# An attention-and-Mish kernel on one core: three kinds of elementwise work move from VectorE to GpSimd, and the written order changes

## The chip, the cores and the metric

The kernel runs on one core of one Trainium2 chip. The metric is device time in microseconds of one execution. Three executions of the kernel before took 684.23, 684.58 and 684.82 us, and the median, 684.58, is the time to compare with. The profile names the engines PE (TensorE matmuls), PEld (TensorE weight loads), DVE (VectorE), ACT (ScalarE), POOL (GpSimd) and SP (the queue that issues most DMAs).

## The reference

```python
def _A_ref(x, wqkv, wo):                       # x: 1 x 2048 x 640, 32 heads of 20 columns
    qkv = (x @ wqkv).reshape(B, S, 3, H, Dh).transpose(2, 0, 3, 1, 4)
    q, k, v = qkv[0], qkv[1], qkv[2]
    p = softmax(einsum("bhqd,bhkd->bhqk", q, k) * Dh ** -0.5, axis=-1)
    return einsum("bhqk,bhkd->bhqd", p, v).transpose(0, 2, 1, 3).reshape(B, S, D) @ wo
def _B_ref(x, w1, b1, w2):                     # 640 -> 1536 -> 640
    h = x @ w1 + b1
    return (h * tanh(softplus(h))) @ w2        # Mish
g = sigmoid((x * gate_w).sum(-1))
return g * _A_ref(x, wqkv, wo) + (1 - g) * _B_ref(x, w1, b1, w2)
```

All inputs and the output are bfloat16.

## The kernel before

The attention is cut into 32 groups. A group is four heads (a "quad", eight of them) and 512 query rows (four chunks). A group has 16 key tiles of 128 keys; a tile times a head is one score unit, so there are 16 x 4 x 32 = 2048 score units. A score matmul (L1119) uses 32 rows of the PE array, so that up to four of different rows run side by side, and it fills one PSUM bank of 128 x 512.

The exponential of a unit is made in one of two ways. In 1380 units ScalarE does it (`x`, L1137), one to three banks in an instruction, into the ring E. In the other 668 units (167 tiles, called `d` sets) VectorE does it by arithmetic on the bits (`power_of`, L615): it writes 16-bit integers which, read as bfloat16, are an approximate power of two. Such an approximation is made better by averaging copies with different offsets. A copy with an offset is an integer addition over the whole set, 128 x 2048 bfloat16 read as 512 words of 64 bits, and GpSimd does it (`add_shift`, L645, two additions for each set, 334 in all). 151 of the sets ("three") keep three copies: the first is multiplied with V (tile VA), the other two with V scaled by a constant (tile VD). The other 16 ("two") let VectorE add two copies (L669) and use two. The set's tiles are nine buffers named T0 to T8 in the code.

The multiplication with V (`V`, L1154) takes four matmuls side by side, one head each, 21 columns wide: 20 of V and a column of ones, so that the sum of the exponentials comes out with the result. It adds up in one PSUM bank, `acc`. When a group's last `V` is done, `normalise` follows: `a` transposes `acc` in blocks of 32 into T1 on VectorE (L1183), `b` takes the reciprocal of the sums (L1190), `c` multiplies 128 x 320 floats of T1 by it into the bfloat16 tile T2 (L1197), and four DMAs store T2 to `o_dram`. For the last two groups of the last chunk a further transpose takes the place of the DMAs or, in the very last group, of `c` also.

VD is made once for a quad: `make_vd` (step `v`) queues two VectorE instructions (L597), one for each constant, over 128 x 588 bfloat16. Seven of a quad's sixteen key tiles have a scaled V. The other work is matrix products in `chains`: q, k and v projections, the hidden layer (48 evacuations with the bias, L882), the second layer (L924) and the output projection (L998). The bias arrives as bfloat16 in `b1bf` and is cast to floats in `b1f` ahead of the first evacuation of the hidden layer (L881).

Nothing is scheduled automatically. The string `ORDER` is the whole program order, the outcome of a search. `S n,bank` makes n score units, `D` one score unit of a `d` set, `x n` an exponential over n banks, `V j,i` the product of tile j (i = -1 from E, 0 to 2 from the copies of a set), `C`, `F`, `f` work on a chain, `d` opens a set. VectorE's and GpSimd's instructions are put into two numbered lists when they become possible (`dve`, `gps`), and `y n` or `p n,tag` emits entry n; the tag says which T buffer an addition writes, or -1 for none or in place. Each engine executes its own instructions strictly in the order in which they were emitted, and waits for semaphores in that order.

Of the kernel before, what the change touches and what calls it, by code (L numbers as in the profile page):

```python
# [19 lines left out]
S2,5 x2 S2,2 S2,0 C0,4 C1,5 C2,6 F0 F0 F0 F0 F0 F1 y1 F y3 x2 C3,5 S1,2 y4 S1,3 C4,6 x2 x2 F3 F S1,0 y5 S1,1  # L20
C6,5 F F d1,2,0 F F y2 F d0,0,0 x2 F S1,3 y6 x1 S1,2 S1,4 F F F F x1 C5,6 F6 F6 F6 F F6 F F F F6 F6 x1 F6 C7,0
F6 F6 F6 C8,4 y7 S3,1 x2 F7 F5 F7 F7 y8 y9 F7 F F7 y10 y12 S2,1 x1 y11 S2,5 V1,-1 F F F F C9,3 d1,7,0 V0,-1 F8
F8 F8 y13 F8 F8 x2 F F8 F8 F8 F8 S3,0 F8 F8 F8 F8 x2 F8 F8 F x3 F F y14 F S2,5 V2,-1 x2 V3,-1 S1,0 y15 S1,1
y16 y17 C11,5 S1,2 y18 y19 S2,3 C10,6 x3 V4,-1 F F11 F11 F11 F11 F11 F11 F F F11 F F S1,1 q1 S1,2 V5,-1 x2 F11
F11 y20 v0,0 F11 F11 F11 F11 S1,0 C12,3 x2 S1,4 D0,15,3,6 F11 F11 F11 F11 F11 x1 F11 F F11 x1 F y23 S2,1
D0,15,0,0 y24 d3,4,0 d0,6,0 y25 y26 y27 F y28 x2 D0,15,2,5 S1,4 y29 S1,6 F V6,-1 F x1 y30 x1 l3 y31 S1,0 S1,2
x1 C13,5 F F S1,6 x1 S1,3 D0,14,3,1 S1,4 C14,0 F13 F x1 F F13 F13 F y32 y33 F F F V7,-1 S2,1 D0,15,1,6 y34 F F
F F x2 F F F F D0,14,0,5 S2,3 V8,-1 F F y35 F F F x2 D0,14,1,6 S2,1 y36 F V9,-1 C15,6 y37 y38 y39 x2 V10,-1
S3,3 x2 F F y40 F x3 F y41 l2 F F F F D0,14,2,2 y22 S2,0 y21 p1,8 V15,0 F F V11,-1 S1,5 y42 S1,3 y43 V14,0 y44
# [308 lines left out]
def kernel(  # L338
# [12 lines left out]
    nc = tc.nc  # L351
# [236 lines left out]
    def make_vd(p, part):  # L588
# [14 lines left out]
        for i in range(NSH):  # L603
            dve(lambda i=i: scale(i))
# [256 lines left out]
    def h_chain(ft, c, start, due):  # L861
# [14 lines left out]
        def evac(ch):  # L876
            ps = ch.ps

            def copy():
                if (ft, c) == (0, 0):  # L880
                    nc.vector.tensor_copy(b1f, b1bf)  # L881
# [563 lines left out]
```

## Time and profile before

| | us | share of the span |
|---|---|---|
| profiled execution | 685.2 | |
| its span (first to last instruction) | 683.4 | |
| PE busy | 674.0 | 99% |
| ACT busy | 667.9 | 98% |
| DVE busy | 603.0 | 88% |
| POOL busy | 356.8 | 52% |

The profiled execution took 685.2 us, of which 683.4 us lie between its first and its last instruction; 0.6 us more than the median of the three timed runs. The granted TensorE clock was 1.000 over the whole span. Busy times of an engine are unions: a matmul's record lasts until its modelled end and overlaps the next one's, so 99% says that PE was never long without a matmul in flight, and not that it streamed at its peak. The groups by line give, for each kind of instruction, the number, the busy time, the mean duration, and the idle time that its engine spent just before instructions of the kind, with what ended it.

### The profile page before, as it was taken

What the parts mean: (1) busy time and instruction counts of PE and PEld (TensorE: products, weight loads), DVE (VectorE), ACT (ScalarE), POOL (GpSimd) and SP (SyncE); (2) the same over time, 40 slices, a digit from 0 to 9 for tenths busy, and PEclk for the clock granted to TensorE, in tenths of its full rate; (3) what the DMA queues carried; (4) which work ended last, traced back from release to release, by engine and by line L of the source; (5) the groups of instructions that cost most, each with busy time, mean ns of one, the idle gap of its engine ahead of it and who ended that gap; (6) DMA issues with size and microseconds to landing.
All of it is one profiled execution on the core that took longest, in us unless ns stands there. A gap on an engine that the chain in (4) does not pass through costs nothing.

```text
span 683.4 us, 24492 instructions
## 1 busy us (share of the span) xinstructions
PE 674.0 (99%) x10339; PEld 236.7 (35%) x10339; DVE 603.0 (88%) x1037; ACT 667.9 (98%) x695; POOL 356.8 (52%) x349
## 2 busy tenths in 40 slices
PE   8999999999999999999999999999999999999997
PEld 4433332323333443333333223222243333333333
DVE  5688989899999889999889988999998988899896
ACT  6999999999999999999999999999999999999995
POOL 5045555454454535575555545456645655565543
PEclk9999999999999999999999999999999999999999
DMA  7443422214312121112132113321322113162231
GB/s 170 99 100 94 89 49 71 49 34 93 74 25 53 38 48 27 26 39 38 44 92 42 34 58 89 46 70 28 58 55 73 19 30 64 25 82 43 56 86 59
DMA packets 128542, 40.47 MB, mean 59 GB/s; under 512 B 94960, under 2 KB 127872, under 8 KB 128432
## 3 DMA queue, kind: packets, MB, share of 16 engines
q1 hardware_dynamic: 126032, 38.29, 25.5%
q8 instruction: 81, 1.33, 0.8%
q10 hardware_dynamic: 2400, 0.62, 0.4%
q14 instruction: 29, 0.24, 0.1%
HBM read 22.29 MB, written 12.78 MB: 51 GB/s over the span
## 4 chain that ended last, share of the span: by engine, by line
PE 81%; ACT 12%; DVE 3%; issue 3%; DMA 1%; POOL 0%; SPq 0%; DVEq 0%; POOLq 0%; ACTq 0%
PE Sp L699 27%; PE Sp L1119 26%; PE Sp L1154 26%; ACT E L1137 12%; DVE T L615 1%; DMA wf<-in_A_wqkv_dram 1%; PE Sp L688 0%; DVE T L669 0%; DVE st L784 0%; DVE T L1197 0%; POOL T L645 0%; PE Sp L1384 0%; PE Sp L1169 0%; DVE ot L1401 0%; PE Sp L1263 0%
## 5 line engine op out<-in xcount | busy, mean ns | idle before, releaser
L1137 ACT ACTIVATE E<-Sp 128x1024 bf16<-128x1024 f32 (+2 forms) x677 | 635.9, 1090 | 3.5 <-PE Sp L1119 2.7
L645 POOL INT64_ADD T<-T x334 | 347.0, 1050 | 311.7 <-DVE T L615 180.1
L615 DVE TENSOR_SCALAR T<-Sp 128x512 int16<-128x512 f32 x668 | 438.1, 684 | 49.8 <-PE Sp L1119 41.0
L1119 PE MATMUL Sp<-qT,kT 32*128 32x512 bf16 x2048 | 260.9, 383 | 1.9 <-DVE T L615 0.9
L1119 PEld LDWEIGHTS <-kT 32*128 32x128 bf16 x2048 | 69.5, 91 | 234.1 <-issue 229.2
L1154 PE MATMUL Sp<-E,VA 128*21 128x512 bf16 x1380 | 129.5, 382 | 0.0
L1154 PE MATMUL Sp<-T,VD 128*21 128x512 bf16 x1272 | 117.6, 382 | 0.1
L699 PE MATMUL Sp<-w_sb,big 128*32 128x320 bf16 x1508 | 77.1, 302 | 0.3 <-DVE T L615 0.2
L699 PE MATMUL Sp<-xT,w1t 128*32 128x512 bf16 x952 | 75.0, 382 | 0.0
L1154 PEld LDWEIGHTS <-VA 128*21 128x21 bf16 x2048 | 44.8, 90 | 62.8 <-issue 55.5
L1154 PE MATMUL Sp<-T,VA 128*21 128x512 bf16 x668 | 64.1, 382 | 0.0
L699 PE MATMUL Sp<-xT,ws 128*32 128x512 bf16 x720 | 56.6, 382 | 0.3 <-DVE VA L838 0.2
L699 PEld LDWEIGHTS <-big 128*32 128x32 bf16 x1508 | 34.0, 95 | 30.3 <-issue 21.2
L1154 PEld LDWEIGHTS <-VD 128*21 128x21 bf16 x1272 | 31.1, 90 | 36.8 <-issue 29.8
L882 DVE TENSOR_SCALAR big<-Sp,b1f 128x512 bf16<-128x512 f32 x48 | 35.6, 742 | 2.2 <-PE Sp L699 1.8
L699 PE MATMUL Sp<-wv,xT 128*32 128x81 bf16 (+2 forms) x960 | 34.8, 257 | 0.0
L699 PE MATMUL Sp<-wo_sb,od 128*32 128x320 bf16 (+1 forms) x604 | 30.3, 300 | 0.0
L699 PEld LDWEIGHTS <-w1t 128*32 128x32 bf16 x952 | 21.5, 94 | 25.2 <-issue 18.0
L784 DVE CAST st<-Sp 128x512 bf16<-128x512 f32 x36 | 24.4, 684 | 2.8 <-PE Sp L699 2.1
L1183 DVE STREAM_TRANSPOSE T<-Sp 128x512 f32<-128x512 f32 x32 | 22.7, 709 | 2.2 <-PE Sp L1154 2.0
L699 PEld LDWEIGHTS <-xT 128*32 128x32 bf16 x960 | 20.6, 96 | 11.3 <-issue 5.9
L699 PEld LDWEIGHTS <-ws 128*32 128x32 bf16 x720 | 17.1, 95 | 19.1 <-issue 12.5
(82 smaller groups left out, 222.5 us busy)
## 6 DMA issues: line engine op xcount, KB each, us to landing
w1t<-in_B_w_dram SPq DMA_DIRECT2D x24, 320.0 KB
q_dram<-st SPq DMA_DIRECT2D x20, 128.0 KB
b_dram<-bt SPq DMA_DIRECT2D x16, 160.0 KB
bl<-b_dram SPq DMA_DIRECT2D x16, 160.0 KB
qT<-q_dram SPq DMA_DIRECT2D x124, 20.0 KB
o_dram<-T SPq DMA_DIRECT2D x120, 20.0 KB
out_dram<-ot SPq DMA_DIRECT2D x15, 160.0 KB
kT<-k_dram SPq DMA_DIRECT2D x28, 80.0 KB
```

The lines of the kernel that those rows point to most:

```text
L615: nc.vector.tensor_scalar(out=dst.bitcast(I16), in0=src, scalar1=inv_sqrt_dh * LOG2E * 128.0, scalar2=127.0 * 128.0 + (BETA2 if two else B ...
L645: nc.gpsimd.int64_add(dst[:, :].bitcast(I64), src[:, :].bitcast(I64), n * 0x0001000100010001)
L699: nc.tensor.matmul(out_[k : k + 32], lhsT=lhsT[:, k : k + 32], rhs=rhs, tile_position=(0, k), start=start, stop=ch.done(), skip_group_chec ...
L784: nc.vector.tensor_copy(out=res["st"][:, :], in_=ps[:, :])
L882: nc.vector.tensor_scalar(out=big[:, pair_of(c, ft), (ft % 2) * QC : (ft % 2 + 1) * QC], in0=ps[:, :], scalar1=b1f[:, ft : ft + 1], scalar ...
L1119: nc.tensor.matmul(ps_cols, lhsT=kT[p][32 * t_ : 32 * t_ + 32, j * P : (j + 1) * P], rhs=qT[G][32 * t_ : 32 * t_ + 32, :], tile_position=( ...
L1137: nc.scalar.activation(E[:, x : x + n, :], allb[:, k0 : k0 + n, :], ACT.Exp, scale=inv_sqrt_dh,)
L1154: nc.tensor.matmul(acc[32 * t_ : 32 * t_ + DH + 1, :], lhsT=lhsT, rhs=rhs, start=(pv_done[G] == 0), stop=(pv_done[G] == pv_total[G] - 1), ...
L1183: nc.vector.transpose(out=st["T1"][:, :, :].rearrange("p b r -> p (b r)"), in_=acc[:, :])
```

## The change

Three things move from VectorE's list to GpSimd's.

- `c` of `normalise`, in 31 of the 32 groups: the product of T1 and the reciprocals (L1197) becomes a GpSimd instruction. It is queued when `b` is emitted, and its DMAs (or the last transpose) follow it as before.
- `scale` of `make_vd`, 16 instructions (L597).
- the cast of the bias, one instruction: it is queued right behind the bias's load (the step `l2`), and no longer stands in the first evacuation of the hidden layer.

```diff
@@ load_late @@
                 nc.sync.dma_start(b1bf, B_b1.rearrange("(ft p) -> p ft", p=P))
+                gps(lambda k: nc.gpsimd.tensor_copy(b1f, b1bf))
@@ make_vd @@
         def scale(i):
-            nc.vector.tensor_scalar(
+            nc.gpsimd.tensor_scalar(
                 out=VD[p][:, lo - (NS - ND) : hi - (NS - ND), i, :],
...
         for i in range(NSH):
-            dve(lambda i=i: scale(i))
+            gps(lambda k, i=i: scale(i))
@@ h_chain @@
             def copy():
-                if (ft, c) == (0, 0):
-                    nc.vector.tensor_copy(b1f, b1bf)
                 nc.vector.tensor_scalar(
@@ normalise @@
         def a_done():
-            dve(b, (lambda: dve(ends)) if G == NG - 1 else (lambda: dve(c, c_done)))
+            dve(b, (lambda: dve(ends)) if G == NG - 1 else (lambda: gps(lambda k: (c(), c_done()))))
...
         def c():
-            nc.vector.tensor_tensor(
+            nc.gpsimd.tensor_tensor(
                 out=T2[i][:, :].rearrange("p (b r) -> p b r", r=32)[:, :, 0:DH],
@@ ORDER, 303 lines become 306; the first of each @@
-S2,5 x2 S2,2 S2,0 C0,4 C1,5 C2,6 F0 F0 F0 F0 F0 F1 y1 F y3 x2 C3,5 S1,2 y4 S1,3 C4,6 x2 x2 F3 F S1,0 y5 S1,1
+S2,5 S1,2 x2 S1,3 C0,4 C1,5 C2,6 S1,0 x2 S1,1 F0 x1 C4,0 F0 F0 F0 F0 y1 F1 y3 F2 C3,5 S2,2 y4 F F4 y5 C6,5
...
```

The steps of the two orders compare as follows.

| steps | before | after |
|---|---|---|
| score units by ScalarE / by VectorE | 1380 / 668 | 1380 / 668 |
| exponentials of 2, 3, 1 banks | 575, 64, 38 | 569, 68, 38 |
| sets with three copies / two copies | 151 / 16 | 149 / 18 |
| `V` steps | 830 | 828 |
| `F` steps, `f` steps | 1210, 40 | 1209, 44 |
| runs of score matmuls (unbroken by another kind) | 640 | 641 |
| VectorE entries `y` | 1006 | 961 |
| GpSimd entries `p` | 334 | 382 |

GpSimd's 382 entries in the changed order are, with `a` for an addition, `n` for the normalising product, `s` for a scaling of V and `b` for the cast:

```
aassaaaabnaaaaaaaaaaaaaaaaaaaanaasnaasaaaaaaaaaaaaaaaanaasaaasaaaaaaaaananaaaaaaaaaaanaasaaaanaaaaaa
aaaaaaaanaaaaaaasaaaanaaaaaaaaanaaaaaaaaaanaaaaaaaaaaaaaaaaannaaaaaaaaaaaaaasaaasaaaaaaananaaaaaaaa
aaaaaaanaaasaaaasaaaaaaasanasanaaaaaanaaaaaaasaasaaaaaaaaaanaaaaaanaaaaaaaaaanaaaaaaaaaaaaaaaanaaaaa
aaaaaaanaaaaaaaanaaaaaaaaaaaaaaaaaanaaanaaaaaaaaanaaaaaaaaaaaanaaaaaaaaaaaaaanaaaa
```

The 47 entries `n` and `s` stand in 44 places between additions (three of them hold two entries each), so the sequence changes 88 times between additions and these two kinds.

More of the change, by code (lines that the diff above doesn't have):

```diff
@@ L25 @@
[L25 to L29, printed above, removed]
@@ new lines @@
+x2 y149 S1,4 D4,13,2,0 C35,5 F y150 F F S2,1 p47,7 x2 D4,11,0,6 F y151 V3,-1 D4,13,3,0 S2,3 x2 V2,-1 x2 V14,1
+S1,1 y152 d5,6,0 S1,2 D4,11,1,6 x2 V13,0 p49,7 y153 F y154 S1,3 D4,12,2,0 S1,4 V14,0 V4,-1 x2 y155 S1,1
+D5,15,0,6 S1,2 x2 V6,-1 V5,-1 p48,1 D4,12,3,0 S3,3 y156 C36,6 y157 V14,2 F F F S2,0 p50,2 D4,11,2,2 F x3 F
+V7,-1 x2 S1,3 p51,0 y158 C37,2 y159 S2,4 F F D4,11,3,6 S2,0 F F V13,1 F y160 x3 y142 S2,3 p52,-1 D5,15,1,5
+y161 V13,2 y162 p54,8 V12,0 x2 V8,-1 y163 S3,0 D5,15,3,6 p55,2 y164 d5,7,0 V11,0 V9,-1 D5,15,2,5 C38,6 x2 S2,3
@@ new lines @@
+x2 F C59,1 F58 F F F d8,5,0 p94,6 S1,2 y264 D8,12,1,0 S1,3 y265 F V13,0 x2 p96,8 p93,-1 F y266 S1,5 D8,12,0,4
+p95,4 S1,6 V14,0 V13,1 y267 S1,1 p97,-1 D8,11,1,0 D8,12,2,3 S1,2 x2 y269 V14,1 V3,-1 C60,3 V5,-1 y268
+D8,12,3,6 y270 x2 S2,4 V14,2 F D8,11,2,2 S1,0 p98,2 S1,1 y271 V4,-1 x2 F S2,4 f60,3 D8,11,0,6 x2 V13,2 x2
+V12,0 f60,2 S1,1 D9,15,1,0 S1,2 y272 x2 y273 V7,-1 F V12,1 d10,8,0 S2,4 D8,11,3,6 f60,0 F p99,4 x2 V12,2 y274
+S1,0 f60,1 S1,1 x2 D9,15,2,2 y275 V6,-1 V8,-1 S1,5 C61,3 y276 D9,15,0,4 S1,6 V11,0 F F S1,0 y277 x2 p100,2
@@ new lines @@
+F80 F85 F85 V14,0 F85 y331 C87,5 p116,8 F86 F86 y334 y332 F80 F86 F V15,2 y333 y316 F86 D10,11,1,6 m y335 F
+F86 y337 C83,4 F87 V12,0 S1,2 C81,0 D10,11,2,1 S1,3 y336 d11,7,1 F87 F83 F83 p118,3 F87 y338 F83 F83 F F F
+p70,-1 D11,15,2,6 y339 C89,5 F83 y341 p117,-1 F81 V5,-1 V3,-1 F81 F F F x2 F F y342 V13,0 y343 S1,0 C69,5
+D10,11,3,4 S1,1 F F F V14,1 x2 F F y344 F F V12,1 S1,2 D11,15,3,4 S1,3 F F x2 F F S1,0 y340 D11,15,0,6 S1,1
+y345 F p122,0 y346 C72,6 V6,-1 x2 S2,2 p123,4 y347 p120,-1 d11,3,1 D11,14,2,4 V11,1 V11,2 q13 p121,-1 p119,8
@@ new lines @@
+D11,12,2,6 C78,5 S2,0 p127,6 F y366 d11,7,1 F F x2 p128,2 F S2,3 x2 x2 D11,11,0,2 d11,0,0 f78,3 F F F
+D11,11,1,6 S2,0 f78,2 y367 F y368 F f78,0 x2 y360 S2,3 D11,11,3,2 p130,8 x2 V13,2 F V2,-1 y369 F D11,11,2,6
+S2,0 f78,1 y371 V3,-1 V13,1 p131,4 x2 y370 D11,10,0,4 S2,2 V12,2 V12,0 y372 D11,10,1,5 S2,0 D11,10,2,6 y373
+C79,5 y374 x2 d12,4,0 V12,1 x2 V5,-1 p132,-1 S1,2 p133,3 S2,3 y375 F F F S1,0 D11,10,3,6 S1,1 x3 y376 V6,-1
+V4,-1 F F F F S1,3 b0 p135,2 d12,1,0 p134,-1 S1,4 D12,15,0,2 y377 V10,0 F x2 F S1,0 x2 S1,1 D12,15,2,6 F F
@@ new lines @@
+D13,15,1,6 S1,1 V11,1 x2 V9,-1 y407 S1,3 D13,15,3,2 D13,15,2,5 S1,4 V10,0 p150,5 y410 x2 V8,-1 y412 S1,0
+p151,7 C90,5 q14 D13,14,1,6 S1,1 V11,2 y411 x2 y413 p152,6 d13,2,0 F F S1,2 D13,14,2,4 d13,0,0 y414 x2 S1,3
+f90,3 F F V10,2 p153,7 D13,13,0,6 S2,0 f90,1 V10,1 x2 x2 F D13,14,3,2 S2,3 f90,2 y415 y416 F F d14,4,0 F F
+S2,0 y417 D13,13,1,6 f90,0 x2 F b1 y419 p154,5 F D13,13,2,4 x2 S1,2 y420 y421 S1,3 V0,-1 V15,0 V15,2
+D13,12,1,5 S1,0 y422 x2 D13,12,0,6 S1,1 V3,-1 d13,3,1 V1,-1 D13,13,3,4 S1,2 x2 S1,3 V15,1 p155,7 C91,5 y423 F
@@ new lines @@
+p173,-1 F y470 F F V10,-1 S2,4 y471 D15,13,2,6 V12,1 F D15,12,1,3 x2 S2,0 p176,0 x2 y472 F F F y474 y473 F
+S1,5 D15,13,3,4 S1,6 F F x2 y476 S2,0 D15,11,0,3 F F x2 y477 k4 p177,3 V0,-1 V14,0 x2 S1,4 p174,8 S1,5
+D15,12,2,6 V15,0 V14,2 S2,0 p178,4 D15,11,1,3 y478 y479 S1,2 V13,0 V1,-1 D15,12,3,6 y481 x2 p175,-1 S2,4 x3
+V14,1 V15,1 V2,-1 V13,1 D15,11,2,6 x2 S1,0 y480 S1,1 p179,8 S1,2 V15,2 p142,-1 V3,-1 x3 S1,3 p180,3 y482
+D15,10,0,5 C98,6 S1,4 V13,2 F F x2 F S2,0 y483 S1,2 D15,11,3,5 y484 V12,0 F V4,-1 F y485 y475 d16,0,0
@@ new lines @@
+D15,10,1,5 p181,7 y486 S1,3 x3 S1,4 V5,-1 V11,0 V12,1 S1,0 D16,15,0,6 S1,1 x2 y487 S1,2 V12,2 x3 C99,5 F F
+p182,6 F S2,3 D15,10,2,6 F d16,4,0 F S1,1 p141,-1 y488 p183,3 D16,15,1,0 S1,2 y489 V7,-1 y490 x2 V11,1 C100,5
+S1,3 x2 S1,4 D15,10,3,6 F F q17 F F x2 D16,14,0,0 S2,1 F F F y491 D16,15,2,6 y492 p185,8 S2,3 F x2 F x2
+d16,5,0 V6,-1 S3,0 V10,0 F F V8,-1 F y493 S1,3 D16,15,3,6 S1,4 y494 p186,1 x3 V11,2 V10,1 V10,2 S2,0 x2
+D16,14,2,5 S1,2 y495 C101,6 F x3 p187,6 F y496 V9,-1 e1 y497 F F F S1,4 D16,14,1,3 S1,5 F F x2 F S2,0
@@ new lines @@
+S1,0 y527 D17,12,0,4 p205,3 y529 S1,1 d17,0,0 V14,0 x2 x2 V1,-1 D17,13,3,6 S1,2 y530 S1,3 V15,1 q18 V2,-1 S2,0
+p203,8 D17,12,1,5 y531 y532 x2 D17,11,0,4 p206,2 V14,2 V14,1 V3,-1 S1,2 x2 y533 S1,3 D17,12,2,6 V13,0 V15,2
+y534 S1,0 D17,11,1,5 S1,1 V4,-1 x2 y528 y535 y536 p207,-1 V13,1 S2,2 C106,5 D17,12,3,6 y537 S1,4 F F x2 F F
+D17,11,2,6 S2,0 V13,2 x3 d18,6,0 F D17,11,3,4 S1,2 y538 S1,3 V5,-1 p209,2 y539 y540 V12,0 V12,1 p210,2
+D18,15,1,6 D18,15,2,5 x2 S1,0 d18,5,0 x2 S1,1 V6,-1 V11,0 p211,3 S1,2 x2 D18,15,0,4 y541 C107,6 y542 S1,3
@@ new lines @@
+C116,6 V4,-1 F F x2 F D19,13,2,5 S2,0 F y589 p228,8 k5 F y590 V14,1 x3 x2 D19,12,0,2 S2,3 V5,-1 D19,12,2,6
+y591 D19,12,1,5 S1,0 y592 S1,1 V14,0 x2 V13,0 p227,-1 p229,2 S1,2 C117,6 x2 S2,3 F y593 x3 p193,-1 F p231,4
+S1,0 D19,12,3,5 p230,-1 y594 S1,1 V13,1 V14,2 F F V6,-1 S1,2 D20,15,1,5 S1,3 x2 S1,4 p232,6 V7,-1 F V13,2 y595
+y596 V8,-1 D20,15,0,5 S2,0 C118,6 V12,0 p233,8 x3 V12,1 S2,2 x2 D20,15,2,4 d20,1,0 y597 F k6 F y598 S2,0
+D20,15,3,5 F F y599 F x2 y600 x2 S1,2 D20,14,1,4 S1,3 V10,-1 y601 V9,-1 S1,0 D20,14,0,5 p234,2 y602 S1,1
@@ new lines @@
+d20,8,0 C119,6 V12,2 x2 F D20,14,2,4 S1,2 y603 S1,3 V11,-1 x2 F S1,0 x2 D20,14,3,5 y604 S1,1 F F y605 p235,6
+S1,2 D20,13,1,4 S1,3 x2 x2 V15,1 F V15,0 S1,0 y607 D20,13,0,5 S1,1 V14,0 p236,2 x2 p237,0 d20,4,0 V15,2 y608
+S1,2 y606 D20,13,2,6 S1,3 y609 V0,-1 V14,1 y610 D20,12,0,4 x2 S1,0 C120,6 S1,1 x2 p239,-1 D20,13,3,5 v7,0
+d20,3,0 V1,-1 F q21 S2,2 x2 y612 y611 F p238,2 F D20,12,3,5 S2,0 F d20,0,0 F V14,2 D20,12,1,4 S1,2 p242,6 x2
+S1,3 V13,1 x2 y613 V13,0 y614 D20,11,3,1 D20,11,0,0 S2,5 y615 V2,-1 V3,-1 S1,3 y616 S1,4 C121,1 d21,7,0
@@ new lines @@
+y663 y664 F S2,0 y666 D22,13,1,5 y667 x2 V15,2 C128,5 V15,0 y665 V0,-1 D22,13,2,6 S2,2 F V15,1 x2 S1,0 p264,3
+D22,12,0,4 S1,1 y668 F F D22,12,2,6 p266,6 x2 p265,7 S2,2 x2 F F S1,0 y669 D22,12,1,4 S1,1 y670 V1,-1 x2
+p267,2 x2 y671 y672 V14,0 S2,2 D22,12,3,6 V14,1 V2,-1 V13,0 y673 p263,-1 S2,0 D22,11,0,4 V3,-1 y674 x2 V14,2
+S1,2 x2 D22,11,2,5 D22,11,3,6 d22,7,0 S1,3 y675 V4,-1 V13,2 S1,0 D22,11,1,4 S1,1 C129,5 F x2 F y676 S1,2
+p268,2 S1,3 D22,10,2,6 y677 x2 d22,4,0 F V5,-1 x2 D22,10,0,4 S2,0 F F S2,2 y678 V13,1 V12,0 V6,-1 x2 x2 y679
@@ new lines @@
+p277,2 F S1,3 d23,3,0 x2 S1,4 D23,14,2,2 F x2 y697 V1,-1 S2,0 D23,13,1,6 V2,-1 F y698 D23,14,3,2 y699 x2 y700
+S2,3 V15,0 V3,-1 V15,1 D23,12,0,5 x2 S1,0 y701 S1,1 D23,12,1,6 V4,-1 y702 V15,2 S2,2 x2 p278,-1 p279,8
+D23,13,2,4 C133,5 F x2 o0,4,5 F S2,0 y703 d23,2,0 D23,11,0,6 x2 F F S2,2 y704 D23,13,3,4 F x2 V5,-1 S1,0
+p280,6 S1,1 D23,11,1,6 x2 H H S1,2 y705 y706 y707 D23,12,2,5 S1,3 V14,2 x2 C137,3 y708 V14,1 S1,0 C134,5
+D23,10,0,6 y709 C140,6 D23,10,1,4 S1,1 p281,8 y710 F134 F134 F134 x2 F134 C144,2 F134 C145,4 q24 F137 F144
@@ new lines @@
+p324,1 S1,1 y817 y816 x2 d27,4,0 p325,2 V10,1 V9,-1 x2 S3,2 y818 D27,14,3,6 x3 C152,5 V10,2 S2,0 F y820 F F x2
+y819 F V0,-1 F S3,2 D27,12,0,6 y822 V15,0 y823 V1,-1 C153,6 D27,14,2,5 S1,0 p326,3 S1,1 V15,1 F x3 F x2 F F
+V2,-1 y824 D27,13,1,5 y825 S3,2 x3 F F F V3,-1 p328,3 F S1,0 D27,13,3,5 S1,1 F q29 y826 F q30 F x2 F
+D27,13,2,4 p329,8 S2,2 V5,-1 V14,1 y827 V14,0 S1,0 D27,12,3,5 p327,1 d28,5,0 S1,1 y828 x2 D28,15,0,6 V14,2
+V15,2 S1,2 y829 S1,3 p330,8 D27,12,1,4 p331,0 x2 d28,1,0 C154,5 V4,-1 F V13,0 d28,2,0 x2 y830 S1,0 D28,15,3,6
@@ new lines @@
+V0,-1 V14,0 D28,13,1,0 S2,3 y848 C158,6 x2 y849 F F y850 V1,-1 S1,1 D28,11,0,5 S1,2 F F x2 y851 S1,3
+D28,13,2,0 S1,4 V2,-1 x2 F p336,-1 F p337,5 S2,1 D28,11,3,5 y844 x2 F F y852 F y853 F S2,3 D28,12,1,0 p338,8 F
+F V3,-1 p340,7 x2 x2 y854 d29,1,0 y855 S1,1 D29,15,0,5 S1,2 V14,2 y856 V13,1 D28,12,2,0 D28,11,1,6 S2,3 x2
+y857 V4,-1 V13,0 p339,-1 S1,1 y858 D29,15,3,5 x2 S1,2 V14,1 d29,8,0 p341,0 V12,0 p342,2 D28,11,2,0 x2
+D29,15,1,6 S2,3 x2 V13,2 y859 V12,1 y860 y861 p343,2 C159,0 p344,7 V5,-1 S1,1 D29,14,0,5 S1,2 F x2 F y862 F
@@ new lines @@
+S1,2 D30,12,2,5 S2,3 V14,0 y908 V2,-1 F V14,1 V13,0 D30,12,0,5 x2 x3 S1,0 p365,4 S1,1 V13,1 V13,2 y909
+D30,12,3,2 S1,6 y910 d30,4,0 x2 C168,5 S2,3 F F F y911 d31,0,0 F F V3,-1 x1 S1,0 y912 S1,1 D30,11,2,6 y913
+S1,2 p366,7 C169,5 V12,0 x2 F F F F F S1,3 x1 S1,4 D30,11,0,6 D30,11,1,0 V4,-1 F x2 F F F y914 S2,1 D30,11,3,6
+y915 F F o3,3,4 p367,1 y916 F x2 d30,2,0 x2 D30,10,0,0 S1,3 d31,6,0 S1,4 x2 V12,1 V6,-1 S1,1 y917 S1,2
+D30,10,3,5 y918 D30,10,2,6 V12,2 V5,-1 p368,5 S2,3 y920 o3,0,3 y919 D30,10,1,0 V11,1 x2 C170,5 V11,0 S1,1
@@ new lines @@
+D31,15,2,6 S1,2 y921 p369,3 V7,-1 V11,2 x2 y922 D31,15,0,0 y923 p370,5 S2,3 p371,7 F x2 F F F F y924
+D31,15,3,6 y925 S1,1 C171,6 S1,2 V8,-1 x2 V10,1 S3,3 x2 D31,15,1,0 V10,0 V10,2 V9,-1 x3 F F y926 S2,1
+D31,14,0,0 p372,4 F d31,2,0 F y927 F y928 V15,0 x2 S1,4 y930 S1,5 D31,14,1,0 S2,1 y931 b11 S1,3 D31,13,0,6
+C172,0 V0,-1 x2 V15,1 F F x3 F b12 F y932 d31,8,0 p373,-1 F S1,4 D31,14,2,6 S1,5 V15,2 y933 D31,13,1,0 S2,2
+C174,1 F F x2 F F F y934 D31,14,3,4 S1,5 d31,0,0 S1,6 V1,-1 y935 V2,-1 y936 C173,1 F F x2 F F S2,2 y937 x2
@@ new lines @@
+D31,12,0,0 D31,13,2,6 y929 x2 S1,4 y938 S1,5 y939 y940 C175,1 V14,0 V3,-1 F F p374,5 F F y941 x2 S1,2
+D31,12,1,0 p375,1 y942 S1,3 V14,1 V14,2 D31,13,3,1 S3,4 C176,0 V4,-1 x2 F F F F y943 F V5,-1 x1 S1,4 y944
+D31,12,2,1 S1,2 C177,0 S1,3 V13,0 F b13 x2 p377,3 y945 F F F D31,11,1,1 x1 S1,4 y946 D31,11,0,6 S1,5 p378,6
+V13,1 y948 V13,2 V6,-1 x2 S1,2 x2 D31,12,3,0 S1,3 y947 C178,6 y949 p376,-1 p379,1 F F F F S1,4 x2 S1,5 V7,-1
+S1,1 y951 x2 p380,3 D31,11,3,0 C179,6 y952 S2,2 F F F F F V8,-1 b14 S1,4 y953 x3 C180,6 D31,11,2,0 S1,5 y954
@@ L320 @@
+V12,1 F V12,2 S2,1 x2 y950 S1,3 F V11,0 V12,0 F C181,0 x3 F180 p381,5 F p382,3 V9,-1 C182,1 y955 V11,1 F181
+F181 F181 C183,3 V10,-1 V11,2 F F182 F F y956 y957 y958 F182 b15 F182 F y959 F182 y961 y960
 """
```

509 lines of the change are left out of this document (215 added, 294 removed).

## The prediction

> **What bounds the kernel now.** I read the page's busy times first, then the shares of the chain that ended last, then the groups by line, and then everything about line 645, because the change puts new instructions between that line's instructions.
>
> ```profile
> span 683.4 us, 24492 instructions
> PE 674.0 (99%) x10339; PEld 236.7 (35%) x10339; DVE 603.0 (88%) x1037; ACT 667.9 (98%) x695; POOL 356.8 (52%) x349
> ...
> PE 81%; ACT 12%; DVE 3%; issue 3%; DMA 1%; POOL 0%; SPq 0%; DVEq 0%; POOLq 0%; ACTq 0%
> ```
>
> PE is without a matmul in flight for 683.4 - 674.0 = 9.4 us, and ACT idles 15.5 us. So two engines are full at once. DVE is at 88% and holds 3% of the chain, 0.03 x 683.4 = 20.5 us; POOL is half empty and not on the chain at all. The groups show how closely POOL nevertheless follows the others:
>
> ```profile
> L1137 ACT ACTIVATE E<-Sp 128x1024 bf16<-128x1024 f32 x575 | 545.7, 1073 | 3.3 <-PE Sp L1119 2.5 <-PE Sp L1154 0.2
> L615 DVE TENSOR_SCALAR T<-Sp 128x512 int16<-128x512 f32 x668 | 438.1, 684 | 49.8 <-PE Sp L1119 41.0 <-POOL T L645 0.7 <-PE Sp L688 0.5
> L645 POOL INT64_ADD T<-T x334 | 347.0, 1050 | 311.7 <-DVE T L615 180.1 <-PE Sp L1154 67.1 <-PE Sp L1119 27.1
> ...
> L1137 ACT ACTIVATE E<-Sp 128x1536 bf16<-128x1536 f32 x64 | 96.6, 1510 | 0.2 <-PE Sp L1119 0.2
> ...
> L669 DVE TENSOR_TENSOR T<-T 128x2048 bf16<-128x2048 bf16 x16 | 20.1, 1254 | 0.2
> L1197 DVE TENSOR_TENSOR T<-T,rec 128x320 bf16<-128x320 f32 x31 | 18.3, 591 | 0.1
> ...
> L597 DVE TENSOR_SCALAR VD<-VA 128x588 bf16<-128x588 bf16 x16 | 6.1, 386 | 0.0
> ...
> L881 DVE CAST b1f<-b1bf 128x12 f32<-128x12 bf16 x1 | 0.2, 165 | 0.0
> ```
>
> The 334 additions have 311.7 us of idle time before them, 0.93 us each, and 180.1 of it ends when DVE finishes a piece of the set: an addition starts when its input is ready. What it makes is also wanted soon. I matched each addition to the first `V` that reads its result, by the order: from the addition's end to that matmul it is 1.5 us in the middle case and 2.1 us on average over 334. The first and the last two in the timeline:
>
> ```profile
> 31.22 1.04 POOL L645 INT64_ADD T<-T  x1 [15.66 <-DVE T L615]
> ...
> 36.36 0.39 PE L1154 MATMUL Sp<-T,VD 128*21 128x512 bf16 x4
> ...
> 672.19 2.06 POOL L645 INT64_ADD T<-T  x2 [0.74 <-DVE T L615]
> ...
> 673.28 0.40 PE L1154 MATMUL Sp<-T,VD 128*21 128x512 bf16 x4
> ...
> 674.34 0.40 PE L1154 MATMUL Sp<-T,VD 128*21 128x512 bf16 x4
> ```
>
> The first result waits 36.36 - 32.26 = 4.1 us. The last two, of 1.03 us each, end at 673.22 and 674.25, and are read 0.06 and 0.09 us later. So POOL is idle half of the time but has hardly any slack: what holds it up for more than about 2 us stops PE. Last, all that line 645 issues:
>
> ```profile
> L645 POOL INT64_ADD T<-T x334: 1032/1039/2000, 31.2 to 673.2; - x167
> L645 POOLq EVENT_SEMAPHORE  x144: 17/17/1932, 34.5 to 672.0; - x144
> L645 POOLq MODIFY_POOL_CONFIG  x2: 7/7/7, 15.6 to 15.6; - x2
> ```
>
> Two MODIFY_POOL_CONFIG stand ahead of the first addition, and none ahead of the other 333. POOL had run only MEMSETs until then, with no such instruction in front, and from the first addition on it runs nothing else:
>
> ```profile
> L1290 POOL MEMSET kT<- 128x2048 bf16 x2 | 3.5, 1802 | 0.0
> ```
>
> So they belong neither to the program's start nor to each addition, but to the step from one kind of instruction to another. I take them for an exchange of the code that POOL holds, one to drop and one to load.
>
> **The change part by part.** *DVE loses* 31 products of 0.591 us (18.3), 16 scalings of 0.386 (6.2) and a cast (0.2), and gains two sums of 1.254 (2.5), as two sets go from three copies to two: -22.2 us, 603 to about 581. By DVE's share of the chain, 22.2 x 20.5 / 603, that is worth 0.75 us, and never more than PE's 9.4 us.
>
> *PE and ACT keep their work.* Two `V` steps fewer and one run of scores more: from the groups of four in these rows a `V` behind a `V` takes 0.21 to 0.22 us, and going into a score run and out of it costs about 0.1 us more each time.
>
> ```profile
> 300.20 0.40 PE L699 MATMUL Sp<-xT,ws 128*32 128x512 bf16 x4
> ...
> 300.42 0.39 PE L1154 MATMUL Sp<-T,VD 128*21 128x512 bf16 x4
> ...
> 300.75 0.39 PE L1119 MATMUL Sp<-qT,kT 32*128 32x512 bf16 x3
> ...
> 301.07 0.40 PE L1154 MATMUL Sp<-E,VA 128*21 128x512 bf16 x4
> ```
>
> -0.4 and +0.4 us: nothing. ACT has 6 exponentials of 1.073 us fewer and 4 of 1.510 more, -6.4 + 6.0 = -0.4 us.
>
> *POOL's own new work.* No row has these instructions on POOL. The product lies between DVE's 0.59 and the 1.04 of an addition over 512 words of 64 bits; I take 0.9. The scaling lies between 0.39 and 1.04; I take 0.8. The cast is 0.17 to 1.04 and runs in POOL's idle time. 31 x 0.9 + 16 x 0.8 = 41 us, 0.93 for each of the 44 places, as much as the idle time before one addition: I cost the arithmetic at nothing, covered by that idle time. Without the cover it is 41 us. The DMAs of a normalised group (four, on SP) follow `c` and come that much later; their data are read groups afterwards. Each moved instruction stands in POOL's queue in front of an addition that it has nothing to do with. A product waits there for the reciprocal, and all additions behind it wait too; they are needed by `V`, `V` by PE.
>
> *The exchanges.* If every step between additions and the moved kinds is an exchange, the order has 88, in 44 pairs. (The cast stands between an addition and a product and adds none.) The price is not visible before, since the one exchange lies in a wait for data. It is bounded: below by the two rows' 2 x 7 ns, above by the 15.6 us from 15.6 to 31.2. The middle is 7.8. The nearest row in kind, a table that ACT loads, is far shorter:
>
> ```profile
> L903 ACT ACT_TABLE_LOAD x2 | 2.6, 1283 | 0.0
> ```
>
> I take 7.0 us, a little below the middle, and keep 0.01 and 15.6 as ends; as likely bounds I use 5.5 and 9.
>
> [...]
>
> *What a pair of exchanges costs PE.* A pair and the work between delay the next addition by 2 x 7.0 + 0.93 = 14.93 us. Three things are taken off: the 0.93 us for which POOL would have idled there; the 2.1 us of an addition's average lead over its reader; and lead that POOL wins back in between, since 334 / 44 = 7.6 additions follow on each other from pair to pair, with 7 us of pauses that shrink while POOL is behind and inputs lie ready. Of these 7 us I give 1.4, one and a half pauses, because PE stalls too and then makes no new inputs. 14.93 - 0.93 - 2.1 - 1.4 = 10.5 us; the cover for the exchanges alone is 3.5 us. Who waits: `V` on PE for the copies, behind it the scores in PE's order, behind these ACT's exponentials and DVE's approximations.
>
> *The sum.* 44 x 10.5 = 462 us on the profiled span: 683.4 + 462 = 1145 us, and 1.8 us around it (685.2 - 683.4), 1147. The profiled execution is 0.6 us above the median; against the median it is 684.6 + 462, or 1146. Counted the other way, POOL would be busy 356.8 + 41 + 88 x 7.0 = 1014 us, which fits into 1145 with 131 us of pauses.
>
> **The rivals.** *No exchange: one load serves all kinds.* For it: MEMSETs needed none, and the page shows no more than the one pair. Then the change does what its diff says. DVE's 22.2 us are worth 0.75 us by the chain's share, and an order with other stalls perhaps 1 to 2 more of the 9.4: 684.6 - 2.5 = 682, faster. It ends on this side as long as an exchange costs less than the 3.5 us of cover for a pair, so below 1.75 us each.
>
> *No exchange, but a busier queue.* The product on POOL waits for DVE's reciprocal with additions behind it. If each of the 44 places costs PE half a microsecond (the 0.93 us of work and a wait, less a lead that is 0.06 to 4.1 us), that is 44 x 0.5 = 22 us less the 2: 705. Against it: POOL's 311.7 us of idle time.
>
> *Exchanges that are cheap, like ACT's table load.* At 1.28 to 5 us each, a pair costs from nothing to 10 - 3.5 = 6.5 us: 690 to 970.
>
> *Exchanges at the upper bound.* At 15.6 us a pair costs 31.2 - 3.5 = 27.7, and 44 of them 1219: 1903. Against it: the 15.6 us are ended by DVE (the row of the first addition names it), so the load need not have taken so long.
>
> *POOL alone is the bound, all else hidden.* 1014 us of work, 21 us of idle time before the first addition (31.2 less 356.8 - 347.0 = 9.8 of other work) and 9 us behind the last (683.4 - 674.2): 1044. It lies in the forecast's range.
>
> **How the numbers follow.** Exchanges at each step, 5.5 to 9 us each: 0.80. With 5.5 a pair costs 11 - 3.5 = 7.5, so 685 + 330 = 1015, and 930 if the cover is 2 us better; with 9 it costs 14.5 and the time is 1323, or 1360 if the cover is 0.9 us worse: 930 to 1360. Cheap exchanges 0.05, dear ones 0.04, a busier queue without exchanges 0.04, no exchange and the relief as meant 0.07. A measurement of this kernel tells 0.2% (1.4 us) from no change. Of the 0.07, 0.05 is faster by more than that and 0.02 within it; all other cases are slower: 0.93. The range 930 to 1360 alone holds 0.80.
>
> **What would show it.** Right: some 89 pairs of MODIFY_POOL_CONFIG (one pair now) at lines 649 (the additions), 601 and 1199; gaps of several us on POOL after each, not ended by any engine; PE and ACT idle for hundreds of us, with `V` on T and VD released by POOL T L645 (not among PE's releasers now); POOL the largest share of the chain; PE's and DVE's busy times not much changed, apart from DVE's -22 us. Wrong: one pair of MODIFY_POOL_CONFIG, and POOL at some 398 us. The size is wrong if the gap of an exchange is not near 7 us, or if an addition's lead at the pair's start is not near 3.5 us. If POOL's queue is the trouble without exchanges, gaps on POOL end with DVE's reciprocal (L1190, there L1192).

## The result and the profile after

The changed kernel takes 1270.88 us (median of six runs, 1267.55 to 1277.87) against 684.73 us: 1.857 times the time before, interval 1.8522 to 1.8625. That is 586 us more, where 462 were forecast, and inside the stated range. Its profiled execution has a span of 1268.1 us. The page's busy times, and its row of the granted clock in 40 slices:

```profile
span 1268.1 us, 24691 instructions
PE 760.9 (60%) x10331; PEld 243.3 (19%) x10331; DVE 595.3 (47%) x991; ACT 681.1 (54%) x693; POOL 404.2 (32%) x397
...
PEclk9788687768778878778659675576768887878788
```

ACT and DVE have about the work that they had, POOL has 47.4 us more, and PE is busy for 86.9 us more with 8 matmuls fewer; no engine is busy for more than 60% of the span. POOL, with 404.2 us of recorded work, is the emptiest of the four; its loss is in time that no record covers. The views of the three lines of GpSimd instructions name what is issued there:

```profile
L649 POOLq MODIFY_POOL_CONFIG  x90: 1/1/11, 14.8 to 1247.3; - x90
...
L1199 POOLq MODIFY_POOL_CONFIG  x58: 1/11/13, 57.1 to 1239.2; - x58
...
L601 POOLq MODIFY_POOL_CONFIG  x30: 1/1/13, 33.1 to 873.8; - x30
```

90 + 58 + 30 = 178 MODIFY_POOL_CONFIG, 89 pairs of rows where there was one: the first, and one for each of the 88 steps between additions and the two other kinds. The timeline shows what a pair of exchanges, there and back, looks like (columns: start in us, us, engine, line, operation, tiles; in brackets the idle time of the engine before and what ended it):

```profile
108.95 1.04 POOL L649 INT64_ADD T<-T  x1 [0.25 <-PE Sp L1156]
...
111.43 0.24 DVE L1192 RECIPROCAL rec<-T 128x16 f32<-128x16 f32 x1
...
117.13 0.72 POOL L1199 TENSOR_TENSOR T<-T,rec 128x320 bf16<-128x320 f32 x1 [7.14 <-issue]
124.07 2.17 POOL L649 INT64_ADD T<-T  x2 [6.22 <-issue]
125.15 0.61 PE L1156 MATMUL Sp<-T,VD 128*21 128x512 bf16 x4 [10.29 <-POOL T L649]
```

The addition ends at 109.99; the product starts 7.14 us later, though the reciprocal that it needs was ready at 111.67. The next addition starts 6.22 us after the product, and the matmul that reads the addition's result waits 10.29 us on PE. "Issue" as the releaser means that no engine released POOL. The single place that holds a scaling and then a product has one exchange ahead of the two and one behind them, and none between them:

```profile
133.36 1.72 POOL L601 TENSOR_SCALAR VD<-VA 128x588 bf16<-128x588 bf16 x1 [7.13 <-DVE T L619]
135.07 0.72 POOL L1199 TENSOR_TENSOR T<-T,rec 128x320 bf16<-128x320 f32 x1
141.91 2.05 POOL L649 INT64_ADD T<-T  x2 [6.12 <-issue]
```

The scaling does not read what its bracket names, and its 7.13 us are as long as the wait of 7.14 that no engine ended. The groups by line, whose releasers are to be read with the same care, add up all the exchanges and give the new instructions' durations:

```profile
L1139 ACT ACTIVATE E<-Sp 128x1024 bf16<-128x1024 f32 x569 | 546.3, 1045 | 394.7 <-PE Sp L1121 393.7
L619 DVE TENSOR_SCALAR T<-Sp 128x512 int16<-128x512 f32 x668 | 441.2, 685 | 541.7 <-PE Sp L1121 524.9 <-POOL T L649 8.6 <-ACT E L1139 1.0
L649 POOL INT64_ADD T<-T x334 | 344.6, 1040 | 533.4 <-issue 281.2 <-DVE T L619 142.7 <-PE Sp L1156 46.9
L1156 PE MATMUL Sp<-T,VD 128*21 128x512 bf16 x1264 | 137.4, 444 | 474.6 <-POOL T L649 469.6 <-POOL VD L601 4.7
L601 POOL TENSOR_SCALAR VD<-VA 128x588 bf16<-128x588 bf16 x16 | 27.5, 1717 | 107.4 <-issue 78.3 <-DVE T L619 14.5 <-DMA kT<-k_dram 7.6
L1199 POOL TENSOR_TENSOR T<-T,rec 128x320 bf16<-128x320 f32 x31 | 22.2, 717 | 207.1 <-issue 163.9 <-PE Sp L1121 21.1 <-DVE T L619 7.6
```

PE waits 469.6 us for POOL's additions (nothing of the kind before), VectorE and ScalarE wait for PE.

**Where the 586 us went.** I compared the distance between the starts of neighbouring groups of matmuls with the usual distance between groups of the same two shapes in the kernel before (658 us in all for both orders). Before, the distances exceed the usual by 21.0 us together, and none does by more than 1.5 us. After, exactly 44 exceed it by more than 1.5 us, with a sum of 501.8 us, 11.4 each on average. The other distances exceed it by 104.7 us, 84 more than before. PE's busy time grew by about as much, 760.9 - 674.0 = 86.9 us, and I put these down to the clock, which the last run below tests. The same stretch of time in slices of 4 us (columns: the stretch, its length, busy time of PE, PEld, DVE, ACT, POOL, then granted clock, DMA share, GB/s):

```profile
116.00:120.00 4.00, 0.00 (x0) 0.00 (x0) 0.00 (x0) 0.53 (x1) 0.72 (x1) 0.68 0.19 12
120.00:124.00 4.00, 0.00 (x0) 0.00 (x0) 0.00 (x0) 0.00 (x0) 0.00 (x0) 0.50 0.22 41
124.00:128.00 4.00, 2.85 (x27) 0.69 (x26) 0.69 (x1) 0.71 (x1) 2.07 (x2) 0.50 0.00 0
128.00:132.00 4.00, 4.00 (x38) 0.68 (x31) 2.22 (x4) 2.51 (x4) 0.00 (x0) 0.61 0.01 2
```

While PE idles, its granted clock falls to 0.50 (this trace's clock records hold 1.00 and 0.50 and nothing between), and it is still at 0.50 when the matmuls come back at 125.15; in the last slice, at a mean clock of 0.61, there are 38 matmuls. Two slices of the kernel before, the ones with the most and the fewest matmuls of five neighbours, from 110 to 130 us:

```profile
118.00:122.00 4.00, 4.00 (x69) 1.49 (x61) 2.98 (x5) 4.00 (x5) 2.63 (x4) 1.00 0.33 96
...
126.00:130.00 4.00, 4.00 (x55) 1.16 (x51) 3.91 (x8) 4.00 (x5) 2.24 (x3) 1.00 0.38 31
```

So a pair of exchanges costs on average 11.4 us of stall and 84 / 44 = 1.9 us of slow matmuls behind it, 13.3 in all.

### The profile page after: what moved, and what is told of

Same layout as the page of the kernel before. It is cut to its first block, busy times and chain, and to the rows that moved or that the text cites. A ratio compares the mean times of both kernels' runs of the same rounds, so it can differ in the third digit from the quotient of the medians.

```text
span 1268.1 us, 24691 instructions
## 1 busy us (share of the span) xinstructions
PE 760.9 (60%) x10331; PEld 243.3 (19%) x10331; DVE 595.3 (47%) x991; ACT 681.1 (54%) x693; POOL 404.2 (32%) x397
## 5 line engine op out<-in xcount | busy, mean ns | idle before, releaser
L1139 ACT ACTIVATE E<-Sp 128x1024 bf16<-128x1024 f32 (+2 forms) x675 | 649.0, 1064 | 574.2 <-PE Sp L1121 573.0
L649 POOL INT64_ADD T<-T x334 | 344.6, 1040 | 533.4 <-issue 281.2
L1156 PE MATMUL Sp<-T,VD 128*21 128x512 bf16 x1264 | 137.4, 444 | 474.6 <-POOL T L649 469.6
L1121 PE MATMUL Sp<-qT,kT 32*128 32x512 bf16 x2048 | 281.9, 418 | 13.8 <-DVE T L619 12.7
L1156 PE MATMUL Sp<-E,VA 128*21 128x512 bf16 x1380 | 139.5, 410 | 0.0
L1199 POOL TENSOR_TENSOR T<-T,rec 128x320 bf16<-128x320 f32 x31 | 22.2, 717 | 207.1 <-issue 163.9
L703 PE MATMUL Sp<-xT,w1t 128*32 128x512 bf16 x948 | 88.0, 442 | 0.0
L703 PE MATMUL Sp<-w_sb,big 128*32 128x320 bf16 x1504 | 83.7, 322 | 0.0
L1156 PE MATMUL Sp<-T,VA 128*21 128x512 bf16 x668 | 71.7, 424 | 11.8 <-DVE T L619 11.8
L601 POOL TENSOR_SCALAR VD<-VA 128x588 bf16<-128x588 bf16 x16 | 27.5, 1717 | 107.4 <-issue 78.3
L673 DVE TENSOR_TENSOR T<-T 128x2048 bf16<-128x2048 bf16 x18 | 23.3, 1295 | 48.5 <-POOL T L649 48.5
```

The source lines that it names most:

```text
L601: nc.gpsimd.tensor_scalar(out=VD[p][:, lo - (NS - ND) : hi - (NS - ND), i, :], in0=VA[:, j0 : j0 + hi - lo, 4 * p : 4 * p + 4, :].rearrang ...
L649: nc.gpsimd.int64_add(dst[:, :].bitcast(I64), src[:, :].bitcast(I64), n * 0x0001000100010001)
L673: nc.vector.tensor_tensor(out=d[0][:, :], in0=d[0][:, :], in1=d["T"][:, :], op=ALU.add)
L703: nc.tensor.matmul(out_[k : k + 32], lhsT=lhsT[:, k : k + 32], rhs=rhs, tile_position=(0, k), start=start, stop=ch.done(), skip_group_chec ...
L1121: nc.tensor.matmul(ps_cols, lhsT=kT[p][32 * t_ : 32 * t_ + 32, j * P : (j + 1) * P], rhs=qT[G][32 * t_ : 32 * t_ + 32, :], tile_position=( ...
L1139: nc.scalar.activation(E[:, x : x + n, :], allb[:, k0 : k0 + n, :], ACT.Exp, scale=inv_sqrt_dh,)
```

## The experiments

The theory is that the exchanges on GpSimd are the whole loss, about 13.3 us a pair. Rival A is the order (additions queued behind unrelated waits, and a changed sequence for all engines). Rival B is the arithmetic, slower on GpSimd. Later runs ask whether any foreign instruction breaks the run of additions, and why the clock falls.

**The same order, products and scalings on VectorE** (`e1_all_on_vector`).

```diff
-            nc.gpsimd.tensor_tensor(          # c
+            nc.vector.tensor_tensor(
...
-            nc.gpsimd.tensor_scalar(          # scale
+            nc.vector.tensor_scalar(
```

> The changed kernel, with the products of the normalising and the scalings of V issued on VectorE again, at the same places of the changed order; only the cast stays on GpSimd. No exchange is left (one pair of MODIFY_POOL_CONFIG). Theory (the exchanges of GpSimd's code are the whole loss): 680 to 690 us, no stall of PE over 1.5 us, clock 1.0. Rival A (the searched order, with additions queued behind unrelated waits, is the loss): well over 1000 us.

Measured: 699.39 us (697.85 to 700.36), 1.0201 of the kernel before, interval 1.0186 to 1.0217. The view of the additions' line in this run:

```profile
L649 POOLq MODIFY_POOL_CONFIG  x2: 6/6/6, 17.5 to 17.5; - x2
```

571 of the 586 us are gone with the 88 exchanges, and rival A as the main cause is out. What stays, 14 us, is outside what I expected: this order with its work back on VectorE is slower than the old one. The run with copies below bears on that.

**Scalings alone, and products alone, on GpSimd** (`e2_scale_only`, `e3_norm_only`): one of the two edits of the run above at a time, so that 15 or 30 pairs of exchanges stay.

```diff
 # e2_scale_only
-            nc.gpsimd.tensor_tensor(          # c
+            nc.vector.tensor_tensor(
 # e3_norm_only
-            nc.gpsimd.tensor_scalar(          # scale
+            nc.vector.tensor_scalar(
```

> The changed kernel with the products back on VectorE and the 16 scalings on GpSimd: 15 pairs of exchanges in place of 44. Theory: the loss goes by pairs, 586 / 44 = 13.3 us each, so 685 + 15 x 13.3 = 885 us. Rival B (the loss is the slow arithmetic on GpSimd, 27.5 us of scalings and 22.2 us of products): 27.5 / 49.7 of the loss stays, 685 + 324 = 1009 us.

> The changed kernel with the scalings back on VectorE and the 31 products on GpSimd: 30 pairs of exchanges. Theory: 685 + 30 x 13.3 = 1084 us. Rival B (arithmetic): 22.2 / 49.7 of the loss stays, 685 + 262 = 947 us.

Measured: 897.12 us (894.32 to 897.76) and 1082.91 us (1081.3 to 1088.17). The additions' line, of the first run and then of the second:

```profile
L649 POOLq MODIFY_POOL_CONFIG  x32: 6/7/11, 14.8 to 652.3; - x32
```

```profile
L649 POOLq MODIFY_POOL_CONFIG  x62: 1/1/6, 14.7 to 1065.3; - x62
```

These are the first pair of rows and one for each of 15 and of 30 returns to additions. The scalings are the longer work (27.5 us against 22.2) and the cheaper move. Over the 699.39 us without exchanges these are 197.7 / 15 = 13.2 and 383.5 / 30 = 12.8 us a pair; for the changed kernel it is 571.5 / 44 = 13.0. (The 699.39 us hold work on VectorE that the changed kernel does not have there; over the kernel before it is the 13.3 from above.) Rival B, with 1009 and 947 us, is out.

**The same products in fewer places** (`e7_merged_norm`). As `e3_norm_only`, with seven products moved in the order to stand right ahead of the next group's.

```diff
 # ORDER; groups 1, 4, 6, 8, 10, 14 and 18: the step p of c(G) moves to stand in front of the step p of c(G + 1)
```

> The run with the 31 products alone on GpSimd, with seven of them held back until the next group's product, so that both stand together: the same 31 products in 23 places in place of 30. Theory: 1083 less 7 x 12.8 = 993 us. If the loss went by the number of products, or by the work behind them: 1083 us, no change.

Measured, with the first pair of rows and one for each of 23 returns to additions:

```profile
L649 POOLq MODIFY_POOL_CONFIG  x48: 1/1/6, 15.1 to 977.1; - x48
```

The time is 1001.42 us (1000.43 to 1005.78), 81.5 us less than with 30 places, 11.6 for each of the seven, somewhat less than the 12.8 expected. The number of places counts, with the same 31 products and the same arithmetic.

**Exchanges without work, in the old order** (`e4_small_scale`). Nothing is moved. One column is scaled into a scratch tile, 44 times. (The sequence of GpSimd's entries printed further up lacks one `a` in its second row; the places here are counted in the order itself, with all 334 additions.)

```diff
+    side = consts.tile([P, 1], F32, tag="side")
...
+        "z": lambda: nc.gpsimd.tensor_scalar(
+            out=side[:, :], in0=warm[:, :], scalar1=2.0, scalar2=None, op0=ALU.mult
+        ),
 # ORDER of the kernel before: a step z behind additions 2, 6, 26, 28, 30, 46, ... 316, 330, as in the changed order
```

> The kernel before, with 44 scalings of a single column (128x1 floats into a scratch tile, read by nobody) put into GpSimd's queue, each behind as many additions as the 44 places of the changed kernel. Nothing else is moved. Theory: 44 pairs of exchanges with next to no arithmetic, a stall of about 10.5 us and 1.9 us of slower clock each, 685 + 44 x 12.4 = 1230 us. Rival A (order) and rival B (arithmetic): 685 to 700 us.

Measured: 1239.75 us (1234.61 to 1242.07), 1.8077 of the kernel before (1.8031 to 1.8123). The group of the 44 instructions, and below it what the additions' line issues:

```profile
L1362 POOL TENSOR_SCALAR side<-warm 128x1 f32<-128x1 f32 x44 | 11.4, 260 | 326.2 <-issue 267.0 <-DVE T L616 37.8 <-PE Sp L1120 14.1
```

```profile
L646 POOLq MODIFY_POOL_CONFIG  x90: 6/7/7, 15.9 to 1219.1; - x90
```

11.4 us of work that nobody reads cost 554 us, 12.6 for each of the 44. Neither the order nor the arithmetic is needed for the loss.

**The same places, another kind of instruction** (`e5_small_copy`).

```diff
-        "z": lambda: nc.gpsimd.tensor_scalar(
-            out=side[:, :], in0=warm[:, :], scalar1=2.0, scalar2=None, op0=ALU.mult
-        ),
+        "z": lambda: nc.gpsimd.tensor_copy(side[:, :], warm[:, :]),
```

> As the run before with 44 small instructions in the old order, but each is a copy of the single column in place of a scaling. The bias cast of the changed kernel, an instruction of this kind, had no MODIFY_POOL_CONFIG at it. Theory: no exchange, 44 short instructions in GpSimd's pauses, 685 to 687 us. Rival (any instruction between the additions breaks their run): 1240 us, as with the scalings.

Measured: 685.28 us, 0.9998 of the kernel before (0.9989 to 1.0007).

```profile
L1362 POOL COPY side<-warm 128x1 f32<-128x1 f32 x44 | 9.5, 216 | 0.0
```

```profile
L646 POOLq MODIFY_POOL_CONFIG  x2: 6/6/6, 15.0 to 15.0; - x2
```

No exchange, no idle time ahead of a copy, no loss. It is the kind of instruction that decides in these runs: 44 copies stand between the additions with the 2 rows of the kernel before, and so does the bias cast of the changed kernel (0.19 us, no such row at its line), while the scalings and products of the changed kernel have 30 and 58 rows at their lines.

**The change without its exchanges** (`e6_copies`).

```diff
         def c():
-            nc.gpsimd.tensor_tensor(
-                out=T2[i][:, :].rearrange("p (b r) -> p b r", r=32)[:, :, 0:DH],
-                in0=st["T1"][:, :, 0:DH],
-                in1=st["rec"][:, :].unsqueeze(2).to_broadcast([P, NS, DH]),
-                op=ALU.mult,
-            )
+            nc.gpsimd.tensor_copy(
+                T2[i][:, :].rearrange("p (b r) -> p b r", r=32)[:, :, 0:DH], st["T1"][:, :, 0:DH]
+            )
 # scale: likewise tensor_copy(VD..., VA...)
```

> The changed kernel with its order, but the products and the scalings on GpSimd are plain copies between the same tiles (the multiplications by the reciprocals and by the constants are left out). That is the change with its work on GpSimd and without exchanges. Theory: 680 to 690 us, no stall over 1.5 us; it shows what the order was searched for. Rival A (additions behind unrelated waits): 750 us and more.

Measured: 684.69 us (683.61 to 686.37), 0.9997 of the kernel before, interval 0.9988 to 1.0007: no difference. Its page and its groups on GpSimd:

```profile
PE 672.4 (99%) x10331; PEld 235.8 (35%) x10331; DVE 588.7 (86%) x991; ACT 666.6 (98%) x693; POOL 377.5 (55%) x397
```

```profile
L648 POOL INT64_ADD T<-T x334 | 345.6, 1044 | 289.2 <-DVE T L618 161.4 <-PE Sp L1155 52.9 <-PE Sp L1120 27.5
L1198 POOL CAST T<-T 128x320 bf16<-128x320 f32 x31 | 13.9, 452 | 0.0
L601 POOL COPY VD<-VA 128x588 bf16<-128x588 bf16 x16 | 10.7, 674 | 0.4 <-DVE z_t L849 0.4
```

The copies leave out the multiplications and the wait for the reciprocal, and are 25 us shorter on GpSimd than the real instructions, so this run is a lower bound for a GpSimd without exchanges. So even if products and scalings needed no exchange, the change would be worth nothing measurable: VectorE is relieved, and PE and ACT are as full as before. The run also bears on the 14 us of the first one: this order takes 14.7 us more with the work on VectorE than with copies on GpSimd (699.39 - 684.69), and the old order did the work on VectorE without such a loss. Which waits make up the 14.7 us was not followed up.

**PE kept busy in the stalls** (`e8_heat`). The changed kernel, with products and scalings where it has them. A step `H` is four matmuls by a tile of zeros.

```diff
 # ORDER: 50 steps H ahead of 42 of the 44 matmul steps that had waited for an exchange
+H H H ... (50 times)
```

> The changed kernel with 50 extra steps of four matmuls by zero weights (0.213 us a step, 10.7 us) ahead of 42 of the 44 matmuls that waited for an exchange. They fill the stall and change no result. Theory (TensorE's clock falls to half because PE idles in the stalls, and that is 84 of the 586 us): the clock stays near 1.0, some 80 us are won and some 20 lost where the stall is shorter than the filling, about 1210 us. Rival (the clock falls because of the exchange or of the memory traffic, not of PE's idling): clock near 0.77 as before, 1290 us or more.

Measured: 1246.53 us (1242.64 to 1256.74), 24 us less than the changed kernel although 8400 matmuls were added. The mean clock of the profiled execution is 0.963 in place of 0.772. The groups of the fillings and of the matmuls behind exchanges:

```profile
L1209 PE MATMUL Sp<-xT,zero_w 128*21 128x512 bf16 x8424 | 462.8, 379 | 0.0
...
L1194 PE MATMUL Sp<-T,VD 128*21 128x512 bf16 x1264 | 121.8, 395 | 74.9 <-POOL T L687 74.6
```

By the same comparison of distances as above, between the two profiled executions (1268.1 and 1254.9): the long stalls fell from 501.8 to 81.7 us and the fillings took 454 (0.216 a step, where 0.213 had been put), which is 34 us lost; the excess of the other distances fell from 104.7 to 58.2 us, 47 won. The exchanges stay as many (90 rows at the additions' line in both), so the clock falls because PE idles, and not because of the exchange itself. I had expected about 60 us in all: the filling lost 34 us where I had put 20, and 37 of the 84 us put down to slow matmuls stayed. The clock was not full all the time: a mean of 0.963 over 1254.9 us is half speed for some 93 us, if this run's clock also has the changed kernel's two values of 1.00 and 0.50, which is worth 46 us at most. Whether that is all of the 37 us I did not follow up, so that 47 of the 84 us are shown to be the clock's, and the rest is not.

## Why the prediction was right

- *The count.* 88 exchanges in 44 pairs were read off the order. There are 178 MODIFY_POOL_CONFIG, and PE has exactly 44 stalls of over 1.5 us. The reading of two 7 ns rows as an exchange tied to the kind of instruction, the step on which all rested, is confirmed by the pair of runs with scalings and copies of one column (90 rows and 1239.75 us, 2 rows and 685.28 us). That the rows exchange code is the prediction's reading of their name: the runs show the rows, the idle time and the kinds of instruction that bring them, and not what is loaded.
- *The price of an exchange*, 7.0 us between 0.01 and 15.6. From MODIFY_POOL_CONFIG to the start of the instruction it is 7.07 us in the middle case for products (6.70 to 7.64), 7.09 for scalings, 6.02 for going back to additions (5.5 to 7.2). A pair is some 13.2 us where 14.0 were taken. That it came so near is luck in part: the trace before left everything from 0.01 to 15.6 us open, and 7.0 was taken as a little below the middle. No row of before shows the 7.0, or the 5.5 and 9 that were taken as likely bounds.
- *GpSimd's own work.* 0.717 us a product (0.9 taken) and 1.717 us a scaling, outside the bounds of 0.39 to 1.04: the nearest rows were no bound here. In all 49.7 us, not 41. The work was costed at nothing, as covered by POOL's idle time. Where there are no exchanges the run with copies, 24.6 us of work, agrees. Beside the exchanges the cover is doubtful: the 44 scalings of one column, with 38 us less work than the change, cost 554 us and not 586, 32 us less, though in the other order.
- *The cover.* 14.93 - 10.5 = 4.4 us were taken off a pair. With 13.2 + 49.7 / 44 = 14.3 us of POOL's time and 11.4 of stall it was 2.9. So POOL's time for a pair was taken 0.6 us too high and the cover 1.5 us too high, and the stall came out 0.9 us too short, which is 0.9 x 44 = 40 us. The term that I chose most freely, 1.4 us of lead won back, has about the size of the error in the cover, but no run tells the three terms of the cover apart.
- *The term that was missing.* The sum had no place for PE's clock. What was put down to it above is 84 us, and with the 40 that is the whole difference between the forecast of 1146 and 1271 us; 47 of the 84 are shown by the run with the filled stalls. The fall shows in the slice from 120 to 124 us, at 0.50: PE's last matmul ahead of that stall ended at 114.87 us, and the clock's record of 0.50 starts at 117.44, 2.6 us later. In the 37 of the 44 stalls in which such a record starts, it starts 1.3 to 4.9 us after the last matmul, 3.0 in the middle case. The return takes longer. In the stall shown, a mean of 0.61 from 128 to 132 us is half speed until about 131 us, some 6 us after the matmuls came back at 125.15, and by the trace's clock records the return came 3.2 us after the end of a stall at the earliest and 4.9 in the middle case of the 44. An estimate from that middle case is 4.9 x 0.5 = 2.4 us for a stall, if PE had work all that time; 1.9 were measured on average.
- *VectorE's relief*, 0.75 us by the chain's share, 2.5 with the new order. With copies in place of the moved work, and so without exchanges, the change measured 0.9997 of the time: nothing. As far as copies stand for it, the rival "no exchange" would have come out as no change and not as 682. VectorE's busy time fell from 603.0 to 595.3, and to 588.7 where nothing stalls, not to 581, since durations that were added up overlap in part: in the trace before, the 48 moved instructions cover 18.4 us that no other VectorE record covers, where 24.7 were added up.
- *What was to be seen.* Gaps on POOL ended by no engine, and PE waiting for POOL T L649, as forecast. That POOL would lead the chain could not be checked: the page's chain of this execution breaks off at its last instructions.

## What to carry to other kernels

An engine that is half idle is not free for every kind of work. Ask which instructions it already runs, whether the new ones bring an exchange on it (in these traces, a pair of MODIFY_POOL_CONFIG rows of 1 to 13 ns at each step between additions and products or scalings, and 6.0 to 7.1 us in the middle case until the instruction behind it starts), and how often the order would go back and forth: here 50 us of work brought 88 exchanges and 586 us. If two such kinds must share GpSimd, put equal ones together; seven places fewer were worth 81 us. And a stall on TensorE can cost more than its length: here the matmuls behind a stall of 11.4 us ran at half the clock (0.50) at first, and 1.9 us more were lost on average.

## What the runs showed of the hardware that was not expected

- TensorE's granted clock falls to 0.50 in a stall of some 10 us and is still there when the work returns; up to 1.9 us are added to a stall of 11.4, of which filling the stalls won back 47 / 44 = 1.1.
- A scaling by one constant, 128 x 588 bfloat16, takes 1.72 us on GpSimd, and a copy between the same tiles 0.67. On VectorE the scaling took 0.39.
- 44 copies of one column in GpSimd's queue between additions cost nothing (0.9998 of the time); 44 scalings of one column cost 554 us.
- In the one place where a product follows a scaling, no exchange stands between them: the product starts at 135.07 us, as the scaling ends (133.36 + 1.72).
